# Reciprocals of softmax sums: two VectorE transposes, or 128x32 numbers and small DMAs

## The chip, the cores and the metric

The kernel runs on one NeuronCore of one Trainium2 chip. The metric is device time in microseconds (us) of one execution, the median of the runs. Five engines work side by side, each through its own list of instructions in order: TensorE (PE in the profile, with its weight loads as PEld), VectorE (DVE), ScalarE (ACT), GpSimd (POOL) and SyncE (SP). SP computes nothing here: it issues nearly all DMAs, one after the other, and an issue that has to wait holds up every issue behind it.

## The reference

Two independent parts, joined along the last axis.

```
a: qkv = x @ wqkv                       x (2048, 576), 32 heads of 18
   scores = q.k / sqrt(18), key j allowed for query i if 0 <= i - j < 256
   o = softmax(scores) @ v
   a = concat_heads(o) @ wo
b: K = real part of sum over n of C * exp(dt*A*l) * dt*B     (576 channels, 2048 taps)
   b = causal convolution of u (2048, 576) with K along the sequence + u * Dskip
out = concat([a, b], -1)                (2048, 1152)
```

What matters here is the division in the softmax: each head and query has one sum of exponentials, and the 18 numbers of that head's output are divided by it.

## The kernel before, in words

The kernel is written as *streams*, Python generators named by a letter, and the order of all work is a string in `PLAN`. One letter runs the next step of a stream; a letter with a digit runs the next posted continuation of that kind. Every engine executes its instructions in the order in which the string makes them, and the semaphore waits between engines follow from which tile each step reads or writes. Nothing is reordered at run time. There are four strings: `front` and `tables` (projection of q, k, v and the taps of the convolution), `first`, and `rest`, in which attention, the convolution by its spectra and the output projection are interleaved. The change is in `rest`.

Attention works on 16 *items*, item i = 4c + o being a block c of 512 queries and a group o of 8 heads. Per item:

- `aload` (stream L, `load`): SP loads Q, K and V of an item from DRAM into one of three sets of buffers. This is done for item i + 3 once item i has been through `o_out`.
- `smax` (stream s): 16 score tiles for the row maximum on PE (L836, and the mask L844), each reduced by DVE (`red`, L870). The 16 columns are transposed on PE (L852), scaled by DVE into `m16` (L856), and four small DMAs of 2 KB (L863) write them into a row of the Q tile, so that the following score matmuls subtract the maximum.
- `scores` (stream a): the scores again, with that row (L921) and the mask (L930), and the exponential by ACT (L936).
- `pv` (stream v): PE multiplies by V (L956). V carries a column of ones times a constant, so in each group of 32 output rows, rows 0 to 17 are a head's output and row 18 is its softmax sum. ACT copies the result to SBUF (`osb`, 128 x 1024, L966).
- `norm` (stream n): the division, as below, then a split into a high and a low half (L994, L998) and four stores to DRAM (`od`, L1003). Once the four items of a query block are stored, the stream `wo` loads them for the output projection.

PE, DVE and ACT share three PSUM slots (`ring`): a score tile holds one from its first matmul until DVE or ACT has read it. The convolution uses the same slots: loads `tx` and `tk` (stream k, L660), spectra on PE (L675), products on DVE (L690, L691) and POOL (L696, L697), inverse on PE (L708), stores `h` (L721), reloads `hp` (L758) and a last transform (L769).

The division before: for each item DVE transposes all of `osb` in 32x32 blocks (L981), which puts the 32 sums of each partition into column 18; takes the reciprocal of that column, 128x32 numbers (L983); and transposes a broadcast of the reciprocals back (L985), so that every row of a group of 32 has the group's reciprocals. POOL multiplies (L990).

Of the kernel before, what the change touches and what calls it, by code (L numbers as in the profile page):

```python
# [10 lines left out]
F32 = mybir.dt.float32  # L11
# [31 lines left out]
def constants():  # L43
# [23 lines left out]
    for nm, v in mult.items():  # L67
# [40 lines left out]
        "a1vc2asaa1a1s6Lavva1sc3aa1ss2s2svs2ss4saa1s2s2ssas2s2sa1kss2s2nvvn3aa1kcc1aa1dc2sad1s2sksvs2s2a1v1cc"  # L108
        "1dc3dc2d4d1d1nc3cc1avc2ln1ksvs2vad4a1sn6ls2ss2a1vasaa1vs2Lla1ssvas6s2vsks2a1sdvss2as4n3n1s2d1sa1ac3s"
        "a1s2n6ss2ss2lan4d4a1ss2vsvv1ss2s2as2a1ss2vcc1c2ss2dd1aa1sc3s2svsLaa1s2vs2ala1vsaa1ss6sss2s2vas2ss2ss"  # L110
        "2vna1n3kn4aaa1a1vcvc1s4c2ass2a1vaa1vsd4ssv1s2s2s2aa1n1sc3vsss2s2s2Ldcnd1ac1c2dvd4a1sss2d1akva1sd4s2s"
        "2vd4asc3a1s2dslld1s6kn6ss4sas2s2svs2a1ss2savs2ss2a1sas2vd4a1sass2n3s2va1n1n6ss2sas2vsa1as2a1ss2ss2vL"
        "cllv1c1aaa1a1vvc2ss2ss2fakva1aa1sfavss6a1c3ee1s2saa1s2dcd1e4vvnc1c2aavvc3a1sa1s2s4aasfvs2kla1a1slvs2"
        "v1Ln4n4cc1c2elsve1vs2ss2asa1s2saa1ss2ss2asn3s2a1ss2s2ss2ss2svvalc3s2cn1lla1c1aa1ad4nvvc2n3ssa1ss6as2"
        "s2a1vss2as4ssve4a1s2ss2avs2asa1a1ds2svad1s2a1n6ssc3s2s2sas2sv1a1vvaas2a1a1snn3s2vvdss2d1asss2s2a1fvk"
        "kLcc1d4c2vaa1dd1sss6n4s2ass2va1aa1ess2ve1ss4s2ss2avn1ss2a1d4ass2ss2vLa1sn6ss2c3ekv1ss2s2sn1s2e1asa1s"
        "2sss2s2van4a1cdc1and1vvc2sac3va1s2ss6n3ss2a1saas2sa1a1s2svskvn1ss2as2d4svs2s2a1sas4s2n6sa1vs2assa1vv"
        "s2sd4s2s2ss2v1aaa1a1sss2s2n4vaa1svs2alLa1ss6dn6d1cc1vaa1vnan3c2va1c3ss2aa1s4ss2sss2s2svs2aa1svss2aws"
        "a1s2vase4s2aa1s2a1vvn4se4v1cs2c1aaa1vvc2a1Lsks2savsn1s2s2ss2a1kasvsd4a1s2aa1s2c3vssss6s2avss2ss2s2a1"
        "dsas2s4vd1saa1a1s2svss2s2ss2aan6vn4sa1a1svs2sLs2dsv1s2sd1s2s2asd4s2va1aavsa1aa1a1vs2cc1nd4vc2aavva1s"  # L120
        "sfs6s2fa1an3ea1e1cc1navkc3ln3s4a1c2n1en6e1ss2vsss2n1s2ss2vaa1sc3s2vv1sas2a1dd1ava1ncac1c2dc3va1kaLsd"
        "1aa1a1vs2ss2vaka1ss2svss2s2asvs2ss2a1n6n4asvs2a1sava1s2ss6lss2cc1s4svslvv1s2c2sas2a1d4fd4ln3sls2ss2s"
        "s2s2asas2a1a1e4ssss2s2s2aa1Lsvn4ss2s2savn1vks2safs2a1vasa1a1s2ndd1ss6s4ee1d4ss2vsasa1s2vn6asc3s2s2la"
        "1svs2cdc1d1c2ss2sas2e4sn3n1a1vsas2s2aa1va1ss2ss2c3d4vkss2e4av1sn6van4s2a1svaa1a1s2lsss2vs2clc1c2dd1e"
        "sd4ae1s6vkna1cc1c3c2vadvaa1d1c3a1cvc1vawn3n1n6s4wa1c2w1aa1aa1dc3avd4a1vv1n4n4de4d1vvnd1d4d4aaa1a1waa"
        "1w4wwww1w4w1wwffww1w4aaa1vva1ee1e4ee1faavva1n3w4a1aa1www1wwwww4wwvvw1w4fn1n6w1vvv1ee4nn3w1e1w4wn1ee1"
        "n4ww4www1w4wn6n4wwww1w4w1wwww4e4e4ww1ww4w1wwwww4w1w4w1w4ww1w4",
# [3 lines left out]
class Kernel:  # L131
# [108 lines left out]
    def prep(self):  # L240
        nc, t, sp, tp = self.nc, self.t, self.p["tabc"], self.p["prep"]
        self.halfpi = sp.tile([128, 1], F32, name="halfpi")
        nc.vector.memset(self.halfpi, math.pi / 2)
        src, T, h, r = {}, {}, {}, {}
        for n in ("re", "im"):
# [538 lines left out]
    def att_setup(self):  # L784
        nc, a, ap = self.nc, self.a, self.p["att"]
# [12 lines left out]
        self.od = self.p["dram"].tile([4, 288, 2, 2, 512], F16, name="od")  # L798
        self.loaded = self.maxed = self.ndone = 0
# [174 lines left out]
    def norm(self):  # L974
        nc, np_ = self.nc, self.p["n"]
        for i in range(16):
            c, o = divmod(i, 4)
            yield "DVE", lambda: (self.osb[i],), lambda: i in self.osb and self.ndone >= i - 1
            osb = self.osb[i]
            T = np_.tile([128, 32, 32], F32, name="T")  # L980
            nc.vector.transpose(T.rearrange("p k r -> p (k r)"), osb.rearrange("p z c -> p (z c)"))  # L981
            R = np_.tile([128, 32], F32, name="R")
            nc.vector.reciprocal(R, T[:, :, 18])  # L983
            rb = np_.tile([128, 2, 512], F32, name="T")
# [218 lines left out]
```

## Time and profile before

| | us |
|---|---|
| median of 3 runs | 883.62 (881.54 to 885.16) |
| the profiled execution, its own time | 884.13 |
| its span, first to last instruction | 882.3 |
| PE busy in the span | 724.2 (82%) |
| DVE busy | 599.7 (68%) |
| ACT busy | 522.7 (59%) |
| POOL busy | 378.0 (43%) |
| mean granted TensorE clock | 0.92 |

The profile lists each engine's busy time, groups of equal instructions with what ended the idle time ahead of them, the waits by who waited for whom, and a chain: the work that ended last, followed back from the end, each piece to what released it. A row of a timeline gives the start, the length, the engine, the line, the operation and the tiles; a bracket at its end is the idle time before it and what ended that. SP's rows (SPq) are issues: the length is that of the issue, not of the transfer.

### The profile page before, as it was taken

The page shows a single profiled execution, that of the slowest core. Times are in us where ns is not written, and L with a number is a line of the kernel's source. Part 1 is how long each engine was busy: PE and PEld are TensorE (multiplying, and loading weights), DVE is VectorE, ACT ScalarE, POOL GpSimd, SP SyncE. Part 2 cuts the span into 40 slices and gives each one's busy share as a digit, 9 for nine tenths or more (in the row PEclk, how much of TensorE's full clock was granted, in tenths as well). Part 3 has the DMA queues.
Part 4 walks back from the last instruction along what each step waited for, and adds up shares of the span by engine and source line. Part 5 has one row for each costly group of instructions (what it writes and reads, how often), then busy time and mean ns, then how long its engine had stood idle before and what let it go on. Part 6 is the DMA issues. An engine that isn't in the chain of part 4 may idle for free.

```text
span 882.3 us, 32024 instructions
## 1 busy us (share of the span) xinstructions
PE 724.2 (82%) x14234; PEld 440.0 (50%) x14234; DVE 599.7 (68%) x798; ACT 522.7 (59%) x685; POOL 378.0 (43%) x295
## 2 busy tenths in 40 slices
PE   4565957998889789886888888887998987999977
PEld 2321523456446545454555554455555554567655
DVE  5855887887987787768657796575876767861010
ACT  3247676678777857671455566555766666676421
POOL 2256867766687655665015142221332042432020
PEclk9885969999999999996889999869999999999998
DMA  9795261546247745458549667637639573846743
GB/s 310 256 230 137 61 160 34 141 100 175 63 106 199 152 116 161 99 158 233 145 147 293 212 212 232 163 103 240 204 120 270 166 227 116 264 144 181 236 143 129
DMA packets 211051, 150.85 MB, mean 171 GB/s; under 512 B 102698, under 2 KB 191530, under 8 KB 210656
## 3 DMA queue, kind: packets, MB, share of 16 engines
q1 hardware_dynamic: 208896, 144.80, 58.5%
q0 software_dynamic: 2016, 3.99, 1.5%
q8 instruction: 112, 1.84, 0.9%
q14 instruction: 27, 0.22, 0.1%
HBM read 83.50 MB, written 65.11 MB: 168 GB/s over the span
## 4 chain that ended last, share of the span: by engine, by line
PE 46%; DVE 17%; ACT 12%; issue 10%; DMA 6%; SPq 4%; POOL 4%; ACTq 0%; DVEq 0%; POOLq 0%
PE pp L178 9%; PE po L956 7%; PE ring L178 6%; DVE m L870 5%; ACT P L936 4%; PE ring L708 4%; PE ring L921 4%; PE ring L836 3%; PE ring L675 3%; PE ring L575 2%; PE ring L453 2%; PE ring L769 2%; PE ring L465 2%; DMA K<-kz 1%; DVE m L552 1%
## 5 line engine op out<-in xcount | busy, mean ns | idle before, releaser
L870 DVE TENSOR_REDUCE m<-ring 128x2 f32<-128x640 f32 (+4 forms) x256 | 187.7, 779 | 66.6 <-PE ring L844 61.5
L936 ACT ACTIVATE P<-ring,esc 128x1024 f32<-128x1024 f32 (+2 forms) x160 | 166.8, 1060 | 102.3 <-PE ring L930 91.7
L546 POOL TENSOR_TENSOR m<-A,tr 128x1024 f32<-128x1024 f32 x72 | 144.0, 2017 | 79.2 <-DVE m L552 66.7
L956 PE MATMUL po<-P,V 64*32 64x320 f32 (+4 forms) x2816 | 105.7, 369 | 6.3 <-issue 6.3
L836 PE MATMUL ring<-K,Q 54*64 54x320 f16 (+4 forms) x1024 | 82.3, 322 | 26.5 <-DMA K<-kz 8.6
L696 POOL TENSOR_TENSOR Y<-t,t 128x384 f32<-128x384 f32 x24 | 24.0, 998 | 139.2 <-DVE t L691 133.3
L990 POOL TENSOR_TENSOR osb<-osb,T 128x1024 f32<-128x1024 f32 x16 | 37.8, 2362 | 100.6 <-DVE T L985 80.9
L921 PE MATMUL ring<-Q,K 55*64 55x320 f16 (+4 forms) x1408 | 67.7, 270 | 14.1 <-ACT P L936 3.4
L836 PEld LDWEIGHTS <-Q 54*64 54x64 f16 x1024 | 42.8, 109 | 71.7 <-issue 63.4
L998 POOL TENSOR_TENSOR oh<-osb,oh 128x1024 f16<-128x1024 f32 x16 | 34.1, 2130 | 73.5 <-ACT oh L994 73.5
L178 PE MATMUL pp<-xh,wh 128*128 128x512 f16 x180 | 48.6, 401 | 19.0 <-ACT vst L365 9.6
L178 PEld LDWEIGHTS <-wh 128*128 128x128 f16 x324 | 31.7, 101 | 57.1 <-issue 17.6
L844 PE MATMUL ring<-sm,idb 64*64 64x128 bf16 x896 | 56.9, 229 | 1.5 <-issue 1.5
L552 DVE TENSOR_TENSOR m<-m,m 128x1024 f32<-128x1024 f32 x36 | 53.3, 1480 | 4.8 <-POOL m L546 4.7
L956 PEld LDWEIGHTS po<-P,V 64*32 64x32 f32 x2816 | 39.1, 108 | 34.5 <-issue 25.0
L575 PE MATMUL ring<-Q,m 128*32 128x64 f32 x2304 | 42.6, 231 | 16.1 <-DVE m L552 13.4
L921 PEld LDWEIGHTS <-K 55*64 55x64 f16 x1408 | 33.8, 110 | 42.7 <-issue 34.0
L575 PEld LDWEIGHTS ring<-Q,m 128*32 128x32 f32 x2304 | 37.0, 117 | 29.8 <-issue 12.6
L178 PE MATMUL pp<-xh,wl 128*128 128x512 f16 x180 | 49.9, 412 | 0.0
L981 DVE STREAM_TRANSPOSE T<-osb 128x1024 f32<-128x1024 f32 x16 | 19.8, 1235 | 42.7 <-ACT osb L966 42.7
L930 PE MATMUL ring<-tm,idb 64*64 64x128 bf16 (+1 forms) x1152 | 44.9, 213 | 2.9 <-issue 2.9
L527 POOL TENSOR_TENSOR tr<-tr,mab 128x768 f32<-128x768 f32 x18 | 33.6, 1867 | 31.2 <-ACT tr L522 31.1
(162 smaller groups left out, 1570.2 us busy)
## 6 DMA issues: line engine op xcount, KB each, us to landing
gx<-ust SPq DMA_DIRECT2D x16, 576.0 KB
gk<-kst SPq DMA_DIRECT2D x18, 512.0 KB
tx<-gx SPq DMA_DIRECT2D x24, 384.0 KB
tk<-gk SPq DMA_DIRECT2D x24, 384.0 KB
h<-ho SPq DMA_DIRECT2D x48, 192.0 KB
hp<-h SPq DMA_DIRECT2D x12, 768.0 KB
Q<-qz SPq DMA_DIRECT2D x16, 512.0 KB
K<-kz SPq DMA_DIRECT2D x16, 512.0 KB
```

The source lines that it names most:

```text
L178: self.nc.tensor.matmul(ps, u, v, start=(i == 0), stop=(i == len(ops) - 1))
L546: tt(m[part], A[:, ch, a0:a0 + 8].unsqueeze(3).to_broadcast(sh), tr[:, ch, part, 0:8].unsqueeze(2).to_broadcast(sh), op=OP.mult)
L552: self.nc.vector.tensor_tensor(m[0], m[0], m[1], op=OP.add)
L575: nc.tensor.matmul(kp[32 * st:32 * st + 32, j, :], m[:, ch, 32 * term:32 * term + 32], Q[:, ch, term, :], start=(term == 0), stop=(term == ...
L836: nc.tensor.matmul(ps[z:z + 64, b, :n], d["Q"][rr, 2 * b + pp, 64 * qb:64 * qb + 64], d["K"][rr, 2 * b + pp, k0:k1], start=True, stop=Fals ...
L844: nc.tensor.matmul(out, self.idb[rr], self.sm[rr], start=False, stop=True, skip_group_check=True)
L870: self.nc.vector.tensor_reduce(out, x, axis=AX.X, op=OP.max)
L921: nc.tensor.matmul(ps[z:z + 64, b, off:off + w], d["K"][rr, 2 * b + pp, kc:kc + 64], d["Q"][rr, 2 * b + pp, q0:q0 + w], start=(k == 0), st ...
L930: nc.tensor.matmul(ps[z:z + 64, b, 64 * blk:64 * blk + w], self.idb[rr], self.tm[rr, self.MO[kinds]:self.MO[kinds] + w], start=False, stop ...
L936: nc.scalar.activation(P[:, :, lo:hi], ps[:, :, lo:hi], AF.Exp, scale=self.esc)
L956: nc.tensor.matmul(po[32 * p:32 * p + 32, z, q0:q0 + w], V[64 * z:64 * z + 64, kb * 76 + 19 * p:kb * 76 + 19 * p + 32], P[p % 2][64 * z:64 ...
L990: nc.gpsimd.tensor_tensor(osb, osb, rb, op=OP.mult)
```

## The change

For items 0 to 13 (`LR = 14`) the two transposes go. In their place:

1. SP reads row 18 of each group of 32 rows of `osb` by a DMA into a tile `R` of 128x32: 128 pieces of 128 bytes (L986). It is the step `n`, and it waits for ACT's copy into `osb`.
2. DVE takes the reciprocal of `R` in place (step `n5`, L1000).
3. SP stores `R` to DRAM, a row of `rden` of its own for each item (step `n7`, L1003).
4. SP reads each of that row's four parts back, broadcast to 18 partitions, into one tile `rb`, four DMAs of 18 x 4 KB (step `n8`, L1008). They wait until the store has landed, and until POOL has finished with the `rb` of the item before.
5. POOL multiplies `osb` by `rb` as before (step `n3`).

`rb` is one tile for all items, filled with ones at the start by POOL, since rows 18 to 31 of a group are never written. Items 14 and 15 keep the transposes. In the string `rest` only the steps of stream n are moved or added; all other steps keep their order. For items 0 to 13 `n` now stands 1 to 98 steps earlier than before, and the new steps follow it at a distance of some 10, 2 and 8 other steps.

```diff
-        "a1vc2asaa1a1s6Lavva1sc3aa1ss2s2svs2ss4saa1s2s2ssas2s2sa1kss2s2nvvn3aa1kcc1aa1dc2sad1s2sksvs2s2a1v1cc"
+        "a1nvc2asaa1a1s6Lavvn5a1sn7c3aa1ss2s2svn8s2ss4saa1s2s2ssas2s2sa1kss2s2vvn3aa1kcc1aa1dc2sad1s2sksvs2s2"
...
+        self.rden = self.p["dram"].tile([self.LR, 4, 1024], F32, name="rden")
+        self.rb = ap.tile([128, 1024], F32, name="rb")
+        nc.gpsimd.memset(self.rb, 1.0)
...
             osb = self.osb[i]
+            R = np_.tile([128, 32], F32, name="R")
+            if i < self.LR:
+                nc.sync.dma_start(R, osb.rearrange("(p r) z (k c) -> r p (z k) c", r=32, c=32)[18])
+                self.post("5", (R,), lambda i=i, osb=osb, R=R: self.spread(i, osb, R))
+                continue
             T = np_.tile([128, 32, 32], F32, name="T")
             nc.vector.transpose(T.rearrange("p k r -> p (k r)"), osb.rearrange("p z c -> p (z c)"))
-            R = np_.tile([128, 32], F32, name="R")
             nc.vector.reciprocal(R, T[:, :, 18])
             rb = np_.tile([128, 2, 512], F32, name="T")
             nc.vector.transpose(rb.rearrange("p z (k r) -> p (z k) r", r=32), R.unsqueeze(2).to_broadcast([128, 32, 32]))
             self.post("3", (rb,), lambda i=i, osb=osb, rb=rb: self.norm2(i, osb, rb))
+
+    LR = 14
+
+    def spread(self, i, osb, R):
+        nc, rb, row = self.nc, self.rb, self.rden[i]
+        nc.vector.reciprocal(R, R)
+
+        def out():
+            nc.sync.dma_start(row.rearrange("p (k c) -> (p k) c", c=32), R)
+            self.post("8", (R,), back)
+
+        def back():
+            for p in range(4):
+                nc.sync.dma_start(rb[32 * p:32 * p + 18], row[p:p + 1].partition_broadcast(18))
+            self.post("3", (rb,), lambda: self.norm2(i, osb, rb.rearrange("p (z c) -> p z c", z=2)))
+        self.post("7", (R,), out)
```

What this does to the lists of instructions is seen best at three places. Lines after the setup are higher in the changed kernel: its L810, L811, L813, L816 are the loads of Q, K (two of them) and V, its L867 the maxima's small DMAs, its L661 the loads of `tx` and `tk`, its L722 the stores of `h`, its L1042 a load of weights, its L874 the reduce, L691 and L692 the products, L860 the scaling to `m16`. `Q_4388`, `Q_4392`, `Q_4396` are the Q buffers of the three sets, and the same set's K follows its Q.

SP, item 0, before (loads for item 3, then the maxima of item 2):

```order
L660 DMA tk<-gk 128x4x192
L806 DMA Q_4388<-qz 128x2048
L807 DMA K_4389<-kz 128x4x512
L812 DMA V_4390<-vd 128x608
L863 DMA Q_4396<-m_5645 1x16x64 x4
L660 DMA tx<-gx 128x4x192
```

and now:

```order
L661 DMA tk<-gk 128x4x192
L986 DMA R<-osb 128x1x32
L810 DMA Q_4388<-qz 128x2048
L811 DMA K_4389<-kz 128x4x512
L816 DMA V_4390<-vd 128x608
L1003 DMA rden<-R 128x32
L1008 DMA rb<-rden 18x1024 x4
L867 DMA Q_4396<-m_5650 1x16x64 x4
L661 DMA tx<-gx 128x4x192
```

The read of the sums stands ahead of the three loads, and the store and the four broadcasts ahead of the maxima of item 2.

DVE, items 0 and 1, before (the products of the convolution, the reduces, the transposes):

```order
L856 TENSOR_SCALAR m_5645<-ring 32x128
L870 TENSOR_REDUCE m<-ring 128x2 x9
L981 STREAM_TRANSPOSE T<-osb 128x1024
L983 RECIPROCAL R<-T 128x32
L985 STREAM_TRANSPOSE T<-R 128x1024
L690 TENSOR_TENSOR t_5950<-X,ring 128x768
L691 TENSOR_TENSOR t_5951<-X,ring 128x768
L870 TENSOR_REDUCE m<-ring 128x2 x3
L690 TENSOR_TENSOR t_6084<-X,ring 128x768
L691 TENSOR_TENSOR t_6085<-X,ring 128x768
L981 STREAM_TRANSPOSE T<-osb 128x1024
```

and now:

```order
L860 TENSOR_SCALAR m_5650<-ring 32x128
L1000 RECIPROCAL R<-R 128x32
L874 TENSOR_REDUCE m<-ring 128x2 x9
L691 TENSOR_TENSOR t_5955<-X,ring 128x768
L692 TENSOR_TENSOR t_5956<-X,ring 128x768
L874 TENSOR_REDUCE m<-ring 128x2 x3
L691 TENSOR_TENSOR t_6089<-X,ring 128x768
L692 TENSOR_TENSOR t_6090<-X,ring 128x768
L691 TENSOR_TENSOR t_6158<-X,ring 128x768
L692 TENSOR_TENSOR t_6159<-X,ring 128x768
L1000 RECIPROCAL R<-R 128x32
```

Item 0's reciprocal stands right behind `m16` of item 2; item 1's behind one more pair of products than its transposes did.

SP, item 1, before (a weight load, then the loads for item 4):

```order
L721 DMA h<-ho 128x2x192 x2
L1018 DMA wraw_6226<-in_wo_dram 128x720
L806 DMA Q_4392<-qz 128x2048
L807 DMA K_4393<-kz 128x4x512
L809 DMA K_4393<-kz 128x4x256
L812 DMA V_4394<-vd 128x912
```

and now:

```order
L1003 DMA rden<-R 128x32
L722 DMA h<-ho 128x2x192 x2
L1042 DMA wraw_6229<-in_wo_dram 128x720
L1008 DMA rb<-rden 18x1024 x4
L810 DMA Q_4392<-qz 128x2048
L811 DMA K_4393<-kz 128x4x512
L813 DMA K_4393<-kz 128x4x256
L816 DMA V_4394<-vd 128x912
```

The loads for item 4 now stand behind the store and the broadcasts of item 1.

SP, item 6, before (`hp`, two rounds of convolution loads, the loads for item 9):

```order
L780 DMA out_dram<-y 64x4x192 x2
L758 DMA hp<-h 128x8x192
L660 DMA tx<-gx 128x4x192
L660 DMA tk<-gk 128x4x192
L660 DMA tx<-gx 128x4x192
L660 DMA tk<-gk 128x4x192
L806 DMA Q_4388<-qz 128x2048
```

and now:

```order
L781 DMA out_dram<-y 64x4x192 x2
L986 DMA R<-osb 128x1x32
L1003 DMA rden<-R 128x32
L759 DMA hp<-h 128x8x192
L661 DMA tx<-gx 128x4x192
L661 DMA tk<-gk 128x4x192
L661 DMA tx<-gx 128x4x192
L661 DMA tk<-gk 128x4x192
L810 DMA Q_4388<-qz 128x2048
```

Here the read of the sums and the store of the reciprocals follow each other directly, ahead of five loads.

More of the change, by code (lines that the diff above doesn't have):

```diff
@@ L112 @@
[L112 to L126, printed above, removed]
@@ L128 @@
+        "ww1w4aaa1vva1ee1e4ee1faavva1n3w4a1aa1www1wwwww4wwvvw1w4fn1n6w1vvv1ee4nn3w1e1w4wn1ee1n4ww4www1w4wn6n4"
+        "wwww1w4w1wwww4e4e4ww1ww4w1wwwww4w1w4w1w4ww1w4",
 }
```

22 lines of the change are left out of this document (18 added, 4 removed).

## The prediction

> **What bounds the kernel now.** I read the busy times by stretch first, then the chain of waits, then the timelines of SP, DVE and PE around the steps that move. The steps concerned run from 450 to 785 us, and this is most of that stretch:
>
> ```profile
> 430.00:760.00 330.00, 281.16 (x8058) 171.21 (x8050) 241.72 (x321) 199.33 (x208) 92.26 (x65) 0.94 0.67 200
> ```
>
> After its length come the busy times of PE, PEld, DVE, ACT and POOL. PE has 281 of 330 us. DVE has 242, so it is not the bound; what it delays is a PE that finds no free `ring` slot. PE's own rows in the list of waits give the size of that:
>
> ```profile
> PE ring L836 <- DVE m L870: 3.9, 15, 0.4
> PE ring L921 <- DVE t L691: 2.9, 3, 1.4
> ```
>
> Some 7 us in all, whatever the reason DVE was late. PE executes a fixed list, so a tile that arrives late stops all of it; the question is whether the new waits on SP make tiles late.
>
> **What the change removes.** By the groups of instructions on `T`, each transposed item costs DVE 1.23 + 0.35 + 1.25 = 2.83 us:
>
> ```profile
> L981 DVE STREAM_TRANSPOSE T<-osb x16: 1221/1234/1246, 463.9 to 838.6; 128x1024 f32<-128x1024 f32 x16
> L983 DVE RECIPROCAL R<-T x16: 353/354/356, 465.2 to 839.8; 128x32 f32<-128x32 f32 x16
> L985 DVE STREAM_TRANSPOSE T<-R x16: 1245/1245/1247, 465.6 to 840.2; 128x1024 f32<-128x1024 f32 x16
> ```
>
> The reciprocal stays at about 0.35 us (same size, contiguous instead of strided), so 14 items free 14 x 2.48 = 35 us of DVE. What counts is how much stood on the chain:
>
> ```profile
> 510.07 1.16 DVE T L981
> 511.64 0.49 DVE T L985
> ...
> 586.16 1.16 DVE T L981
> 587.73 0.86 DVE T L985
> ...
> 632.25 1.16 DVE T L981
> 633.83 0.36 DVE T L985
> ...
> 783.44 1.16 DVE T L981
> ```
>
> Four items (2, 5, 7, 13), 6.35 us, and four reciprocals of 0.36 between them: 7.8 us. Elsewhere other work hid the transposes. When they go, the next-longest chain takes over part of it. The gain is between 0 and 7.8 us; I take 6, nearer the chain's own rows.
>
> **What the change adds: prices.** The trace has no DMA of 128 rows by 128 bytes with its landing, but small ones on the same queue appear in the chain, from issue to the work they released, and so do two large loads. Two groups of SP's issues give the issue time (shortest, median, longest):
>
> ```profile
> 594.02 1.87 DMA Q<-m
> ...
> 740.63 4.02 DMA Q<-m
> ...
> 478.82 6.72 DMA K<-kz
> ...
> 461.45 4.21 DMA tk<-gk
> ...
> L863 SPq DMA_DIRECT2D Q<-m x64: 502/587/1515, 414.6 to 787.0; - x64
> L1003 SPq DMA_DIRECT2D od<-oh x64: 264/316/1262, 489.9 to 848.3; - x64
> ```
>
> A small DMA lands 1.87 to 4.02 us after its issue; I take 3.0, the middle, for the read into `R` and for the store to `rden`. The four broadcasts have the shape of the `od` stores (18 rows of 4 KB), so 4 x 0.32 = 1.3 us to issue. The other new issues take 0.3 to 0.6 us. All 84 issues make 84 x 0.32 to 0.59 = 27 to 50 us of SP's time over some 330 us; SP has that on average, and I put nothing for it beside the places below.
>
> The Trainium skill, page "DMA: Bandwidth & Descriptors", section "Anatomy of one DMA — SWDGE (gpsimd) path", puts the fixed cost of a DMA at about 2.0 us, mostly the confirmation that the last byte has landed, from a fit on another issuing path. The small DMAs above agree at their lower end (1.87) and not at their upper (4.02). With 2.0 for 3.0 the sum below would be an estimate of about 6 us smaller.
>
> What the new waits cost depends on the places. `n5`, the reciprocal, stands at a fixed place in DVE's list; `n7` (store) waits for it on SP; `n8` (broadcasts) waits there for the store to land. Everything behind them on SP waits too. I set each place's rows beside the new order.
>
> *Item 0.* The copy into `osb` is early; the reciprocal now stands behind `m16` of item 2 (L856), and that item's maxima behind the broadcasts:
>
> ```profile
> 450.64 1.02 ACT L966 ACTIVATE osb<-po 128x1024 f32<-128x1024 f32 x1
> ...
> 457.38 0.28 DVE L856 TENSOR_SCALAR m<-ring 32x128 f16<-32x128 f32 x1 [0.38 <-PE ring L852]
> ...
> 457.69 3.04 SPq L863 DMA_DIRECT2D Q<-m  x4
> ...
> 461.79 0.50 PE L921 MATMUL ring<-Q,K 55*64 55x64 f16 x12
> ```
>
> SP issues the maxima the moment `m16` is done, and PE starts item 2's scores 4.1 us later, about what such a DMA takes: no slack. Between `m16` and the maxima come 0.35 (reciprocal) + 3.0 (store lands) + 1.3 (broadcasts) = 4.7 us, all of it PE's. Ends 3.5 and 5.7.
>
> *Item 1.* The reciprocal stands behind the pair of products that ends at 480.83; the loads of K for item 4 stand behind the broadcasts:
>
> ```profile
> 479.88 0.95 DVE L691 TENSOR_TENSOR t<-X,ring 128x768 f32<-128x768 f32 x1
> ...
> 477.37 0.43 SPq L806 DMA_DIRECT2D Q<-qz  x1
> 478.16 0.60 SPq L807 DMA_DIRECT2D K<-kz  x1
> 478.82 0.62 SPq L809 DMA_DIRECT2D K<-kz  x1
> ...
> 485.63 0.33 PE L836 MATMUL ring<-K,Q 54*64 54x320 f16 x4 [0.16 <-DMA K<-kz]
> ```
>
> K already arrives 0.16 us late. New issue of its second part: 480.83 + 0.35 + 3.0 + 1.3, and 1.2 for Q and K ahead of it, is 486.7 in place of 478.82: 7.9 us later, of which I count 7.8. Ends 6.7 and 8.9.
>
> *Item 2.* Store, then the loads for item 5, behind a reciprocal that follows the reduce at 500.41:
>
> ```profile
> 500.41 0.82 DVE L870 TENSOR_REDUCE m<-ring 128x2 f32<-128x640 f32 x1
> ...
> 494.44 0.63 SPq L809 DMA_DIRECT2D K<-kz  x1
> ...
> 505.83 0.31 PE L836 MATMUL ring<-K,Q 54*64 54x320 f16 x4
> ```
>
> Reciprocal done at 501.6, store and two loads issued, K's second part at 503.0, landed 6.7 later at 509.7, needed at 505.83: 3.5 rounded down, since loads also land faster. Ends 1.5 and 4.
>
> *Item 6.* The store waits for a reciprocal behind the second of three reduces that start at 610.12, so until 611.3, with five loads behind it:
>
> ```profile
> 610.12 2.52 DVE L870 TENSOR_REDUCE m<-ring 128x2 f32<-128x640 f32 x3 [2.75 <-PE ring L844]
> ...
> 597.55 0.50 SPq L660 DMA_DIRECT2D tk<-gk  x1
> ...
> 612.42 0.50 PE L675 MATMUL ring<-tk,w 64*32 64x192 f32 x7
> ```
>
> `tk` was issued at 597.55, 15 us ahead of its use; it now goes out at 612.8 and lands by the row of 4.21 us at 617: 4.5 us late. Ends 2.5 and 6.
>
> *Items 5, 10, 12.* Here reads or other streams are held:
>
> ```profile
> 579.10 0.34 SPq L1036 DMA_DIRECT2D orow<-omx  x1
> ...
> 576.31 2.52 DVE L870 TENSOR_REDUCE m<-ring 128x2 f32<-128x640 f32 x3 [4.82 <-PE ring L844]
> ...
> 702.28 0.98 SPq L758 DMA_DIRECT2D hp<-h  x2
> ...
> 749.80 0.75 SPq L809 DMA_DIRECT2D K<-kz  x1
> ...
> 759.56 0.33 PE L836 MATMUL ring<-K,Q 54*64 54x320 f16 x4
> ```
>
> Item 5: its read stands behind `orow`, so `R` lands at 579.5 + 3 = 582.5, while DVE reaches the reciprocal among the reduces at 578 and stands for 4.5 us with PE's slots full behind it; part falls in idle time there: 3 (ends 0 and 4.5). Item 10: the `h` stores that `hp` reads back stand behind a store that waits for DVE: 2.5 (ends 0 and 4). Item 12: Q and K of item 15 stand behind the broadcasts; the second K goes out about 5.6 us after 749.80 and lands at 762.1, needed at 759.56: 2.5 (ends 0 and 4).
>
> *Other items, and the rest.* At items 3, 4, 7, 8, 9, 11 and 13 the same working ends within the slack that the loads have: 0, with 1 us each as the upper end. POOL's multiply waits for `rb` up to 9 us longer at item 1, but POOL is busy 92 of 330 us and PE stands there for K anyway: 0. The fill of `rb` at the start is one POOL operation on 128x1024; POOL has room: 0.
>
> Sum: 4.7 + 7.8 + 3.5 + 4.5 + 3 + 2.5 + 2.5 = 28.5, less 6, is +22.5 us. The profiled execution took 884.13 (span 882.3, and 1.8 around it), 0.06% above the median 883.62; 884.1 + 22.5 gives **907 us**. All lower ends with the full gain: 14.2 - 7.8 = +6.4, 890.5. All upper ends without gain: 37.1 + 7 = +44, 928.
>
> **Rivals.** *Faster: SP has the slack.* SP often stands waiting for DVE itself, and what is behind those waits would not notice:
>
> ```profile
> SPq L863 <- DVE m L856: 61.6, 11, 10.3
> ```
>
> If the new waits fall into such time, only the freed DVE time counts: 884.1 - 6 = 878, down to 876 with the whole 7.8 us. Against it: at items 0 and 1 the very thing behind the wait is what PE needs next. It decides from the point where all places together cost PE under 6 us, less than item 1 alone in my count.
>
> *Partly absorbed.* The places do cost, but a late PE gives the next loads slack, and one place pays for several: two places out of seven, say items 0 and 1 at their lower ends, 10.2 - 6 = +4 us, 888.
>
> *Worse.* The large loads ahead of the store in the queue delay its landing as they delay each other (6.72 us for K against 1.87 for a small one). With 6.7 in place of 3.0 at items 0, 1 and 12, where the store must land before the loads go, and 3.7 more at three of the items I put at 0: 907 + 6 x 3.7 = 929.
>
> *No effect from the DVE side.* That the transposes do go is settled by the order of the instructions; that they were hidden is the gain's lower end, and leaves 913.
>
> **How the numbers follow.** I give 0.64 to the forecast (890.5 to 928), 0.09 to the absorbed case, 0.06 to nearly nothing at all, 0.14 to the faster rival and 0.07 to the worse one. About 0.5% (4.4 us) is what a measurement can tell from no change, so faster means below 879.2 and slower above 888. The absorbed case lies at that bound, half to each side. Faster 0.14, same 0.06 + 0.04 = 0.10, slower 0.64 + 0.05 + 0.07 = 0.76. The range of 8 in 10 goes from 881 to 930: it leaves out nearly all of the faster rival and half of the worse one.
>
> **What would show it.** DVE busy lower by some 35 us over the span; DVE no more in the chain with T. In the chain, rows of `rden` and `rb`, and waits of PE on `Q<-m` and `K<-kz` of several us near items 0 and 1, against 0.2 to 4 now. PE's busy time in us unchanged and its share lower. SP's own waits: L1008 on the landing of `rden`, L1003 on DVE's L1000. The forecast is wrong if the scores of item 2 and the first tile of item 4 start as closely behind their loads as now without PE having stood still, or if `R` and `rden` land in under 2 us everywhere.

## The result and the profile after

The changed kernel takes 936.85 us (median of 4 runs, 933.45 to 938.53) against 882.58 for the kernel before on the same chip: ratio 1.061, 95% interval 1.056 to 1.066. It is slower, as forecast, but by 54 us where 22.5 were forecast (907 us), and above the range of 881 to 930. The profiled execution took 936.20 us with a span of 933.8, 51.5 us more than the 882.3 before.

The busy times on the changed kernel's page:

```profile
PE 737.5 (79%) x14234; PEld 448.2 (48%) x14234; DVE 568.1 (61%) x770; ACT 522.7 (56%) x685; POOL 378.6 (41%) x296
```

Against 599.7 before, DVE is relieved of 31.6 us. PE is idle for 933.8 - 737.5 = 196.3 us where it was 882.3 - 724.2 = 158.1: 38.2 us more. And the same 14234 matmuls are busy for 13.3 us longer. These two make the 51.5.

SP's waits between 430 and 860 us, where the items lie (total, times, longest):

```profile
SPq L1003 <- DVE R L1000: 38.5, 11, 6.6
SPq L986 <- ACT osb L970: 32.7, 8, 6.5
...
SPq L1008 <- DMA rden<-R: 27.5, 9, 5.2
...
SPq L867 <- DVE m L860: 8.3, 3, 6.1
```

The first three are new, 98.7 us. They took the place of most of SP's old wait for the maxima's `m16` (61.6 us before, 8.3 now), and some 45 us of them are time that SP did not stand before. PE's waits in the same stretch name what came late:

```profile
PE ring L840 <- DMA K<-kz: 16.4, 5, 7.2
PE ring L925 <- DVE m L874: 8.7, 6, 7.0
...
PE ring L676 <- DMA tx<-gx: 6.6, 2, 5.8
...
PE ring L925 <- DMA Q<-m: 4.6, 8, 1.1
PE ring L840 <- DMA h<-ho: 2.3, 1, 2.3
```

PE's timeline has these stops at the forecast places. The bracket gives the idle time before the row and what ended it:

```profile
462.09 0.63 PE L925 MATMUL ring<-Q,K 55*64 55x64 f16 x3 [0.60 <-DMA Q<-m]
...
494.02 0.48 PE L840 MATMUL ring<-K,Q 54*64 54x320 f16 x4 [7.24 <-DMA K<-kz]
...
519.14 0.48 PE L840 MATMUL ring<-K,Q 54*64 54x320 f16 x4 [4.42 <-DMA K<-kz]
...
603.01 0.64 PE L925 MATMUL ring<-Q,K 55*64 55x256 f16 x8 [6.99 <-DVE m L874]
...
637.85 1.54 PE L676 MATMUL ring<-tx,w 64*32 64x192 f32 x32 [5.77 <-DMA tx<-gx]
```

In order these belong to items 0, 1, 2, 5 and 6. The second row is the one that stood at 485.63 before, with 0.16 us of waiting and a length of 0.33 us. Behind the stop the same four matmuls take 0.48. The stretches around it show the clock (after the length: busy times, then the granted clock, the DMA share and GB/s):

```profile
480.00:486.00 6.00, 5.26 (x162) 2.83 (x170) 4.79 (x7) 2.36 (x4) 2.14 (x1) 1.00 0.36 96
486.00:494.00 8.00, 0.78 (x17) 0.18 (x18) 1.25 (x3) 0.79 (x1) 3.38 (x3) 0.69 1.02 290
494.00:497.00 3.00, 2.98 (x52) 1.45 (x52) 1.02 (x2) 0.79 (x1) 0.86 (x1) 0.50 1.10 336
497.00:500.00 3.00, 3.00 (x56) 2.12 (x52) 1.36 (x2) 0.24 (x1) 0.00 (x0) 0.61 0.69 205
500.00:503.00 3.00, 1.93 (x73) 1.48 (x66) 2.77 (x4) 2.69 (x4) 0.00 (x0) 1.00 0.26 87
```

After the 7.24 us stop PE works 6 us at a clock of 0.50 to 0.61 and loses 1.4 us more: set against the kernel before, instruction by instruction, it is 8.4 us behind at the first tile and 9.8 us behind at 500 us. The Trainium skill, page "TensorE: Matmul & The Clock Gate", section "What's actually happening", says that the clock is halved after an idle window of about 3.4 us and comes back after as long of work. For this stop the trace agrees roughly: the clock is still at 0.50 in the first 3 us of work and back at 1.00 from 6 us on. Stops shorter than that window were followed by the lower clock too (last section), and there the measurement decides.

### The profile page after: what moved, and what is told of

Its sections match the earlier page's. It is cut to its first block, busy times and chain, and to the rows that moved or that the text cites. A ratio compares the mean times of both kernels' runs of the same rounds, so it can differ in the third digit from the quotient of the medians.

```text
span 933.8 us, 32131 instructions
## 1 busy us (share of the span) xinstructions
PE 737.5 (79%) x14234; PEld 448.2 (48%) x14234; DVE 568.1 (61%) x770; ACT 522.7 (56%) x685; POOL 378.6 (41%) x296
## 4 chain that ended last, share of the span: by engine, by line
PE 37%; DMA 17%; DVE 14%; ACT 11%; issue 10%; SPq 7%; POOL 3%; ACTq 0%; DVEq 0%; POOLq 0%
PE pp L179 8%; PE ring L179 6%; PE po L960 4%; ACT P L940 3%; PE ring L709 3%; PE ring L925 3%; DMA K<-kz 3%; PE ring L676 2%; PE ring L840 2%; DMA Q<-m 2%; DVE m L874 2%; PE ring L454 2%; PE ring L576 2%; SPq L867 2%; PE ring L466 2%
## 5 line engine op out<-in xcount | busy, mean ns | idle before, releaser
L874 DVE TENSOR_REDUCE m<-ring 128x2 f32<-128x640 f32 (+4 forms) x256 | 187.0, 778 | 86.5 <-PE ring L848 79.6
L840 PE MATMUL ring<-K,Q 54*64 54x320 f16 (+4 forms) x1024 | 84.2, 332 | 46.7 <-DMA K<-kz 23.6
L925 PE MATMUL ring<-Q,K 55*64 55x320 f16 (+4 forms) x1408 | 69.8, 274 | 24.8 <-DVE m L874 8.7
L1014 POOL TENSOR_TENSOR osb<-osb,rb 128x1024 f32<-128x1024 f32 x14 | 33.0, 2360 | 104.5 <-DMA rb<-rden 54.0
L691 DVE TENSOR_TENSOR t<-X,ring 128x768 f32<-128x768 f32 x24 | 22.9, 954 | 68.0 <-PE ring L676 32.8
L179 PE MATMUL pp<-xh,wl 128*128 128x512 f16 x180 | 47.6, 397 | 0.0
```

What stands on the lines that cost most here:

```text
L179: self.nc.tensor.matmul(ps, u, v, start=(i == 0), stop=(i == len(ops) - 1))
L840: nc.tensor.matmul(ps[z:z + 64, b, :n], d["Q"][rr, 2 * b + pp, 64 * qb:64 * qb + 64], d["K"][rr, 2 * b + pp, k0:k1], start=True, stop=Fals ...
L874: self.nc.vector.tensor_reduce(out, x, axis=AX.X, op=OP.max)
L925: nc.tensor.matmul(ps[z:z + 64, b, off:off + w], d["K"][rr, 2 * b + pp, kc:kc + 64], d["Q"][rr, 2 * b + pp, q0:q0 + w], start=(k == 0), st ...
```

## The experiments

The microseconds below are the ratio to the kernel before on the same chip, less one, times 882.6; by this measure the whole change costs 53.5 (interval 49.1 to 58.0). In code, L1000 and so on are the lines of the changed kernel.

### Is the relief worth anything, and is it waits or traffic?

No small DMA and no transposes:

```diff
-                nc.sync.dma_start(R, osb.rearrange("(p r) z (k c) -> r p (z k) c", r=32, c=32)[18])
-        nc.vector.reciprocal(R, R)
+        nc.vector.reciprocal(self.Rc, self.Rc)
-            nc.sync.dma_start(row.rearrange("p (k c) -> (p k) c", c=32), R)
-            for p in range(4):
-                nc.sync.dma_start(rb[32 * p:32 * p + 18], row[p:p + 1].partition_broadcast(18))
```

> Leaves out, for items 0 to 13, the division by the softmax sums: no small DMA is issued, no transpose is made, the reciprocal works on a constant tile and the product takes ones. So VectorE is relieved as in the change, and nothing is asked of SP. My theory (the gain is the 6 us by which the chain of waits of before stood on transposes, the loss is all SP's): 876 to 882 us against 883 before. Rival (VectorE's work was covered by TensorE and gives nothing): 883. Rival (the lower clock comes from the change of VectorE's work, not from SP): well over 883, and the granted clock near 0.90 as in the changed kernel; by my theory it is 0.92.

Measured: 886.91, ratio 1.0024 (0.9983 to 1.0064), +2.1 us. Its page:

```profile
PE 721.3 (81%) x14234; PEld 439.9 (50%) x14234; DVE 568.7 (64%) x770; ACT 522.5 (59%) x685; POOL 378.3 (43%) x297
```

DVE is relieved as in the change, and the time does not fall. The gain of 6 us, read off four items in the chain, was not there: the interval allows at most 1.5 us. With the other steps at these places, no cheaper way to the reciprocals can gain more than that here, by this interval.

All 84 small DMAs, with no copy, reciprocal or landing to wait for:

```diff
-                nc.sync.dma_start(R, osb.rearrange(...)[18])
+                nc.sync.dma_start(R, self.oc.rearrange(...)[18])
-        nc.vector.reciprocal(R, R)
+        nc.vector.reciprocal(self.Rd, self.Rd)
-            nc.sync.dma_start(row.rearrange(...), R)
+            nc.sync.dma_start(row.rearrange(...), self.Rc)
-                nc.sync.dma_start(rb[32 * p:32 * p + 18], row[p:p + 1].partition_broadcast(18))
+                nc.sync.dma_start(rb[32 * p:32 * p + 18], self.r0[p:p + 1].partition_broadcast(18))
```

> Leaves out the division by the softmax sums for items 0 to 13, but issues all 84 small DMAs at their places on SP's queue with their sizes and addresses alike: the reads take a constant tile, the stores a constant tile, the broadcasts a row written once at the start, and the reciprocal a tile of its own. So SP has the issues and the chip has the traffic, and no wait for a copy of ScalarE's, a reciprocal or a landing. My theory (SP waits, and what is queued behind it comes late): 878 to 890 us, at most 10 us over the kernel without the small DMAs. Rival (the traffic or the time that SP takes to issue 84 DMAs): 920 to 937.

Measured: 887.76, ratio 1.005 (1.001 to 1.010), +4.6 us. Issue time and traffic cost 0.4 to 8.7 us, beside 53.5. The rest is waits, of SP and of DVE.

### Whose waits?

The six small DMAs per item from GpSimd's queue (in all three places):

```diff
-                nc.sync.dma_start(R, ...)
+                nc.gpsimd.dma_start(R, ...)
```

> The changed kernel with its six small DMAs per item issued by GpSimd's queue in place of SP's, at the same places of the program; the output is the whole one. SP's queue is that of before, without waits for reciprocals and landings. My theory (the cost is what stands behind the waiting issues on SP): the late loads of K, Q and h go, GpSimd's own waits delay its products and subtractions, of which little waits, and VectorE still waits for R where it did (3 times, 11.6 us): 885 to 900 us. Rival (traffic, or the late normalisation itself, costs the time): 925 to 940. Rival (GpSimd's queue holds up work that TensorE waits for as SP's did): 910 to 940, with waits of TensorE on GpSimd's tiles in the profile.

Measured: 899.78, ratio 1.018 (1.012 to 1.025), +16.1 us. Some 37 of the 53.5 us (by some 7 us either way) are SP's queue. The Trainium skill, page "DMA: Bandwidth & Descriptors", section "Issuing engines are not separate DMA queues", says that issuing from several engines only saves the sequencer's time. Here the move saved far more than issue time and traffic together can cost (at most 8.7 us, above): the other queue has the same kind of waits, but no loads behind them. Then GpSimd's queue and, besides, no wait of DVE for R:

```diff
-        nc.vector.reciprocal(R, R)
+        nc.vector.reciprocal(self.Rc, self.Rc)
-            nc.gpsimd.dma_start(row.rearrange(...), R)
+            nc.gpsimd.dma_start(row.rearrange(...), self.Rc)
```

> Leaves out the division for items 0 to 13: the small DMAs are issued by GpSimd's queue, and the reciprocal and the store take a constant tile, so that VectorE never waits for R. With both waits away the change would cost little: my theory 884 to 893 (GpSimd's queue alone gave 899.8, and taking VectorE's stand away from the changed kernel gave 13 us by the ratios). Rival (what was left of the cost on GpSimd's queue is the late products and h of GpSimd): 896 to 902.

Measured: 896.06, ratio 1.019 (1.013 to 1.025), +16.9 us. My theory (884 to 893) fell: with the DMAs on GpSimd, DVE's wait for R is worth nothing that these runs can tell. What is left fits the rival, late work of GpSimd, but isn't shown to be that: some 5 us of it may be issue and traffic (4.6 above). In the profile of the former kernel GpSimd's waits are

```profile
POOL rden L1003 <- DVE R L1000: 64.2, 10, 11.5
...
POOL rb L1008 <- DMA rden<-R: 33.4, 12, 5.6
```

with its products and subtractions behind them (from 430 to 860 us). Which of these PE pays for was not taken further.

Each wait alone, on SP's queue as in the change. DVE's wait for R, by the same edit as just now on SP:

> Leaves out the division for items 0 to 13: the reciprocal takes a constant tile in place of R, and the store stores that tile. VectorE then never waits for the landing of R; SP still waits for ScalarE's copy, for VectorE's reciprocal at its place, and for the landing of the stored row. In the changed kernel VectorE stood 11.6 us for R in three places (10.0 of them at item 5), and TensorE 7.0 us behind that. My theory (the prediction's term for item 5, 3 us, was too small: it cost about 9, and without it SP's store of that item goes out earlier too): 923 to 929 against 937. Rival (VectorE's stand hides what comes late anyway): 934 to 938.

SP's wait for the reciprocal:

```diff
-            nc.sync.dma_start(row.rearrange(...), R)
+            nc.sync.dma_start(row.rearrange(...), self.Rc)
```

> Leaves out the division for items 0 to 13: the store takes a constant tile, so that SP doesn't wait for VectorE's reciprocal (38.5 us in 11 places); the reciprocal of R still stands at its place on VectorE, and SP still waits for ScalarE's copy and for the landing of the row. My theory (the three waits of SP each stand for their part of the 37 us that went when the DMAs left SP's queue: 38.5 of 98.7): 14 us less, 920 to 926. Rival (the next wait takes its place: the broadcasts wait for the landing of the row wherever the store goes out): 932 to 938. VectorE's stand for R stays by both.

SP's wait for the landing of the row:

```diff
-                nc.sync.dma_start(rb[32 * p:32 * p + 18], row[p:p + 1].partition_broadcast(18))
+                nc.sync.dma_start(rb[32 * p:32 * p + 18], self.r0[p:p + 1].partition_broadcast(18))
```

> Leaves out the division for items 0 to 13: the four broadcasts read a row that was written once at the start, so that SP doesn't wait for the landing of the row (27.5 us in 9 places); it still waits for ScalarE's copy and for the reciprocal. My theory: 27.5 of 98.7 of the 37 us, so 10 us less, 924 to 930, with the maxima of item 2 back in time (the prediction put 4.7 on store and broadcasts there) and K of item 4 2 to 3 us earlier. Rival (the broadcasts lie behind a wait of SP that lasts as long): 934 to 938.

SP's wait for ACT's copy:

```diff
-                nc.sync.dma_start(R, osb.rearrange(...)[18])
+                nc.sync.dma_start(R, self.oc.rearrange(...)[18])
```

> Leaves out the division for items 0 to 13: the first small DMA reads a constant tile in place of ScalarE's copy, so that SP doesn't wait there for the copy (32.7 us in 8 places), and the read lands earlier, which takes VectorE's wait for R away too. My theory: 32.7 of 98.7 of the 37 us is 12, and VectorE's stand goes with it, some 9: 914 to 920. Rival (SP then waits longer for the reciprocal, which stands behind the copy on VectorE: the wait moves one place on): only VectorE's stand goes, 926 to 932.

| taken away | us, median | ratio (95%) | less than the 53.5, us |
|---|---|---|---|
| DVE's wait for R | 926.71 | 1.046 (1.040 to 1.051) | 13 |
| SP's wait for the reciprocal | 918.22 | 1.038 (1.033 to 1.044) | 20 |
| SP's wait for the landing | 929.83 | 1.052 (1.046 to 1.057) | 8 |
| SP's wait for the copy | 927.97 | 1.049 (1.043 to 1.054) | 11 |

Each difference in the last column is good to some 7 us. The wait for the reciprocal is worth more than that for the landing (no run of one reaches a run of the other); that either is worth more or less than its share of SP's waiting can't be told. The theories held for DVE's wait (923 to 929) and for the landing (924 to 930). For the reciprocal the time came out below both ranges (920 to 926, rival 932 to 938), and for the copy in the rival's (926 to 932). Part of a wait moves on, as the rivals of the last three runs said. SP's list of waits without the wait for the reciprocal shows that for the landing grown from 27.5:

```profile
SPq L1010 <- DMA rden<-Rc: 39.0, 10, 7.4
```

Without the wait for the copy, the list shows that for the reciprocal grown from 38.5:

```profile
SPq L1005 <- DVE R L1002: 70.7, 12, 12.0
```

So of 32.7 us of waiting for the copy almost all went into the next wait. The 11 us are not what the rival named, DVE's stand for R: that was 11.6 us in the changed kernel, and it is still there without the wait for the copy. What they are stays open. Of DVE's waits in that kernel:

```profile
DVE R L1002 <- DMA R<-oc: 12.2, 2, 10.9
```

### Which items?

The kernel with only some items in the new way (the others as before, at their old places in the order), first items 0 and 1:

```diff
-    LR = 14
+    LR = 2
```

> Only items 0 and 1 take the small DMAs, at their new places; items 2 to 15 are written as before. The output is the whole one. The prediction's terms for these two items are 4.7 (maxima of item 2 behind the store and the broadcasts) and 7.8 (K of item 4), 12.5 us together, and the part of the gain that lies in items 0 and 1 is none: 896 us, 893 to 900. The two profiles of before and after, put against each other, give 3.7 and 6.3, so 893. Rival (the loss is spread over all items, by traffic or by the clock): 14 items for 54 us, so 8 us for two: 891, with no wait for K of item 4.

Measured: 895.41, ratio 1.014 (1.008 to 1.021), +12.7 us. The forecast of 12.5 for these two items holds. At the first tile of item 4 PE stands for K, whose second part goes out at 486.36, where the prediction had it (486.7). PE's timeline of this kernel:

```profile
493.62 0.48 PE L839 MATMUL ring<-K,Q 54*64 54x320 f16 x4 [8.40 <-DMA K<-kz]
```

and in SP's timeline of the same kernel K's second part goes out:

```profile
486.36 0.62 SPq L812 DMA_DIRECT2D K<-kz  x1
```

Items 2 to 6:

```diff
-            if i < self.LR:
+            if 2 <= i < 7:
```

> Only items 2 to 6 take the small DMAs, at their new places; the others are written as before, and the output is the whole one. The prediction gave these items 3.5 (item 2), 3 (item 5) and 4.5 (item 6), less about 3 of the gain: 8 us. TensorE's lag behind the kernel before, read instruction by instruction from the two profiles, grows from 8 to 30 us over these items. My theory by now (VectorE's stand at item 5, the loads of items 3 to 6 and a slower TensorE between them cost what the lag shows, and the parts add): 22 us, 900 to 909. Rival (the items only cost so much because the first two had used up the slack): 890 to 898.

Measured: 905.87, ratio 1.030 (1.024 to 1.036), +26.4 us, as my theory had it.

Items 7 to 13:

```diff
-            if i < self.LR:
+            if 7 <= i < 14:
```

> Only items 7 to 13 take the small DMAs, at their new places; the others are written as before, and the output is the whole one. The prediction gave these items 2.5 (item 10) and 2.5 (item 12), less about 3 of the gain: 2 us. The lag grows from 30 to 50 us over them. My theory: 20 us, 898 to 907, and with two items (12.7) and items 2 to 6 (22) the three parts add up to the 54 of the whole change. Rival (a part alone costs much less than in company): 885 to 895.

Measured: 895.18, ratio 1.018 (1.014 to 1.023), +16.2 us, under the 20 of my theory. The three parts make 12.7 + 26.4 + 16.2 = 55.3 us, the whole 53.5; the sum is good to some 9 us, the whole to some 5. Within that the cost adds by places. Single items of the middle part, by the same edit with `if i == 3:`, and then 5 and 6:

> Only item 3 takes the small DMAs, at its new places; the output is the whole one. The prediction gave this item 0, with 1 as its upper end. In the profile with items 2 to 6 two stores of h stand behind the store of its row and land late, TensorE waits 3.0 us for ScalarE's copy of ho that needs their buffer, and the lag grows by about 5, of which some 2 go again. My theory: 3 to 6 us more than before. Rival (only late because item 2 made it so): 0 to 1 us.

Measured: 887.53, ratio 1.0055 (1.0021 to 1.0089), +4.9 us. Of PE's waits in its profile:

```profile
PE ring L924 <- ACT ho L715: 3.8, 2, 3.4
```

What held SP here is the read of the sums, which waits 7.4 us, the last 4.4 of them for ACT's copy. Behind it stand four loads, the store of the row and two stores of `h`. In SP's waits and timeline of this kernel:

```profile
SPq L985 <- ACT osb L969: 4.4, 1, 4.4
...
517.24 0.65 SPq L985 DMA_DIRECT2D R<-osb  x1
520.48 0.38 SPq L1002 DMA_DIRECT2D rden<-R  x1
520.91 1.18 SPq L721 DMA_DIRECT2D h<-ho  x2
```

The store of the row goes out the moment the loads are issued, so it waits for nothing. The two stores of `h` go out at 520.91, at 513.77 in the kernel before. Their buffers come free late, ACT's copy `ho` waits 4.8 us for them, and PE 3.4 us for that copy. The prediction had looked there only for loads, and only behind the store.

> Only item 5 takes the small DMAs, at its new places; the output is the whole one. The prediction gave 3 (VectorE stands for R, whose read goes out late behind the stores of an earlier item; 0 to 4.5). In the profile with items 2 to 6 TensorE waits 8.1 us for VectorE's maxima behind that stand, and the lag grows by 7.5. My theory now: 6 to 9 us more than before. Rival (the read is only late because the other items' small DMAs lie ahead of it): 0 to 3 us.

Measured: 889.58, ratio 1.004 (1.001 to 1.007), +3.7 us. My theory fell, and the prediction's 3 holds, though DVE and PE stand longer than its 4.5 us. Their rows in the list of waits of this kernel:

```profile
DVE R L999 <- DMA R<-osb: 11.7, 1, 11.7
...
PE ring L924 <- DVE m L873: 11.9, 5, 10.7
```

Some 4 us of the stop stand in the place of one in the profile of before, where PE waited for nothing that the profile shows:

```profile
574.84 0.90 PE L956 MATMUL po<-P,V 64*32 64x64 f32 x32 [4.14 <-issue]
```

Instruction by instruction against that profile, PE is level at 570 us, then 4.4 us ahead for want of that stop, and 5.7 us behind after its own; it is 9.1 us behind at 686 us and 4.5 us behind at 749 us.

> Only item 6 takes the small DMAs, at its new places; the output is the whole one. The prediction gave 4.5 (one spectrum load behind the store that waits for the reciprocal; range 2.5 to 6). In the profile with items 2 to 6 the lag grew by about 12 us here, with the loads of tx and tk, of Q, K and V of a later item and two stores of h all behind the same store. My theory now (everything that stands behind the waiting store counts, not only the first): 10 to 13 us more than before. Rival (the prediction's size): 3 to 6 us more.

Measured: 896.19, ratio 1.015 (1.011 to 1.020), +13.2 us, where 4.5 had been forecast. SP's timeline of this kernel:

```profile
603.25 0.64 SPq L985 DMA_DIRECT2D R<-osb  x1
609.57 0.35 SPq L1002 DMA_DIRECT2D rden<-R  x1
610.01 0.38 SPq L758 DMA_DIRECT2D hp<-h  x1
610.45 0.58 SPq L660 DMA_DIRECT2D tx<-gx  x1
611.08 0.50 SPq L660 DMA_DIRECT2D tk<-gk  x1
...
617.64 2.41 SPq L1007 DMA_DIRECT2D rb<-rden  x4
621.07 1.90 SPq L721 DMA_DIRECT2D h<-ho  x2
```

PE's waits in its profile from 595 to 660 us:

```profile
PE ring L675 <- DMA tx<-gx: 6.0, 1, 6.0
PE ring L839 <- DMA h<-ho: 2.6, 1, 2.6
```

The forecast's `tk`, out at 597.55 before, goes out at 611.08 (612.8 forecast). But the stop at these loads is 6.0 us, the stores of `h` behind them make a second one of 2.6, and between the two, from 616 to 619 us, PE has a clock of 0.50. The same with the store behind the loads (`n7` moved past `hp`, `tx`, `tk`, Q, K, V in the order, `n8` to its product):

> As with item 6 alone, but its store is issued behind the loads of tx, tk, Q, K and V that it held up, and its four broadcasts right ahead of their product on GpSimd; the read and the reciprocal stay where they are, and the output is the whole one. My theory (the cost lies in what is queued behind the waiting store): 0 to 3 us more than before. Rival (the cost lies in the reciprocal on VectorE or in the late product): as much as with item 6 alone, 10 to 13.

Measured: 890.57, ratio 1.0063 (1.0031 to 1.0095), +5.6 us. The two waits above are gone (`tx` from the rows, 2.7 us for `ho` in place of `h`), and more than half of the cost with them. The rest is more than my theory gave. The `ho` row is part of it. Another part may be the read, which stands ahead of the loads as before and waits for ACT's copy:

```profile
SPq L985 <- ACT osb L969: 6.9, 1, 6.9
...
604.93 0.50 SPq L660 DMA_DIRECT2D tk<-gk  x1
```

So `tk` still goes out 7 us later than the 597.55 of before. What that wait alone costs was not measured.

### Does another order repair the whole?

The letters of each item's steps moved: read 5 places later, reciprocal 8, store and broadcasts 11 to 14.

> All 14 items take the small DMAs, and the output is the whole one, but each step stands some places later in the order: the read of R 5, the reciprocal 8, the store and the broadcasts 11 to 14, so that most loads of K, V, Q, tx and tk are issued ahead of the stores that wait. My theory (what costs is the waiting in SP's queue, so a later place for the waiting issues takes most of it away): 892 to 910 against 937. Rival (the waits only move to the next loads, of which there are as many): 925 to 940.

Measured: 933.20, ratio 1.058 (1.053 to 1.064), +51.5 us: nearly nothing gained, as the rival had it. SP's waits in its profile:

```profile
SPq L1003 <- DVE R L1000: 38.7, 11, 7.5
SPq L986 <- ACT osb L970: 33.6, 7, 8.5
SPq L1008 <- DMA rden<-R: 20.8, 10, 3.8
```

Together they are nearly as long as before, 93.1 us for 98.7: SP had moved on through its list and waited at the new places as long as at the old. With more room (read 10 places later, reciprocal 20 behind it, store 25 behind that, broadcasts 15, product 16; items 0 to 12):

> As with the first stretched order, but each wait of SP gets more room, in items 0 to 12: the read stands 10 places later, the reciprocal 20 behind the read, the store 25 behind the reciprocal, the broadcasts 15 behind the store, the product 16 behind those; the output is the whole one. The first stretched order left SP's waits as long as they were (38.7, 33.6 and 20.8 us), since 5 places are some 2 us and SP runs further ahead of VectorE than that. My theory (a wait of SP goes only where the place of the issue is later than the work that it waits for): the three waits fall to less than half of the 93 us, and the time to 895 to 912. Rival (later stores and broadcasts hold up other loads, and late products hold up the rest): 920 to 940.

Measured: 903.99, ratio 1.022 (1.017 to 1.026), +19.1 us. SP's waits in its profile:

```profile
SPq L986 <- ACT osb L970: 10.2, 4, 4.5
SPq L1003 <- DVE R L1000: 8.9, 2, 5.5
SPq L1008 <- DMA rden<-R: 7.6, 4, 3.0
```

The three waits fall from 98.7 to 26.7 us and the cost from 53.5 to 19.1, with the same computation and the same DMAs. It is still slower than the kernel before, which fits a relief that is worth nothing.

### Stalls from another engine

The kernel before, with the first transpose made three times:

```diff
-            nc.vector.transpose(T.rearrange("p k r -> p (k r)"), osb.rearrange("p z c -> p (z c)"))
+            for _ in range(3):
+                nc.vector.transpose(T.rearrange("p k r -> p (k r)"), osb.rearrange("p z c -> p (z c)"))
```

> The kernel before, with the first of the two transposes made three times in each of the 16 items: 40 us more of work for VectorE at the places of the normalisation (32 transposes of 1.25 us), no DMA and no wait of SP added. It asks two things: whether the slack of VectorE, by which 32 us less of its work gained nothing, also takes 40 us more, and whether stalls of TensorE that come from VectorE lower the granted clock as those behind SP did. My theory: no slack upward, 15 to 30 us slower (898 to 913), TensorE's busy time up from 724 to some 732 and the clock down to 0.91. Rival (slack both ways): 883 to 888, clock 0.92. Rival (the clock falls by something else): slower by the stalls, with TensorE busy for 724 as before.

Measured: 906.46, ratio 1.031 (1.026 to 1.036), +27.4 us. The busy times on its page:

```profile
PE 728.5 (81%) x14234; PEld 441.8 (49%) x14234; DVE 638.3 (71%) x830; ACT 522.8 (58%) x685; POOL 378.0 (42%) x295
```

32 us of DVE's work taken away gave nothing, 40 us added cost 27, within my theory's 15 to 30. PE's busy time rose by 4.3 us, half of what I expected, with no DMA added.

## Why the prediction was right, and where it was wrong

The direction and the mechanism were right: SP's queue waits for a reciprocal and for a landing, loads behind it come late, PE stands. The size was wrong, and the time lies above the range, by these steps. The stops from item 2 on were priced too low: 11 us for items 2 to 6, which measured 26.4, and 5 us for items 7 to 13, which measured 16.2. Where single items were taken apart, the reasons seen are that only the first load behind the waiting store was counted, that stores of `h` were not, and that the read's wait for ACT's copy was put at nothing. A gain of 6 us was taken off that isn't there. And PE's busy time was put as unchanged, where it rose by 13.3 us at a lower clock.

The rival "SP has the slack" is partly true (some 50 us of the new waits replaced SP's old wait for `m16`), but far from enough. "Partly absorbed" is refuted by the parts, which add. "Worse" had nearly the time, 929, but not the cause: the landing's whole wait is worth 8 us, and what it blamed, a landing behind large loads, shows in the chain of the changed kernel as 5.29 us at most and 2.51 at item 0 (from issue to what it released):

```profile
455.56 2.51 DMA rden<-R
...
687.16 5.29 DMA rden<-R
```

By its terms:

- Items 0 and 1, 12.5: measured 12.7 (6.8 to 18.7). Right, each at its place: instruction by instruction PE's lag grows by 4.6 us at item 0 (4.7 forecast) and by 7.9 at item 1 (7.8 forecast). At item 0 the waits for the maxima are only 0.60 and 0.42 us, since PE came up to them at a clock of 0.50.
- Item 5, 3: measured 3.7 (0.9 to 6.5). Right on the time, and in part by luck: DVE stands 11.7 us for R where 4.5 were forecast, and some 4 us of PE's stop stand in the place of one that the profile of before has. The stop is 7 us long in the whole change and 10.65 with item 5 alone.
- Item 6, 4.5 (2.5 to 6): measured 13.2 (9.3 to 17.2). Mis-sized. I priced the first load behind the waiting store, and not the train behind that load, whose stores of `h` made a second stop. The reciprocal stands behind the first of the three reduces, not the second as written; the 611.3 of the sum is the time for the first.
- "Items 3, 4, 7, 8, 9, 11 and 13: 0": item 3 alone is 4.9 (1.9 to 7.9). I had held only loads against the slack, and only behind the store; here the read waits for ACT's copy, and what comes late is stores of `h`. Item 2, with item 4 and what the items of the middle part do to each other, is left with 26.4 - 4.9 - 3.7 - 13.2 = 4.6 (by some 8 us either way) for a forecast of 3.5.
- Items 10 and 12, 2.5 each, and none for the rest from 7 on: 16.2 (12.4 to 20.0) for the 5. Not measured item by item. In the profile of that part PE waits 4.4 us for `hp` at item 10, above its upper end of 4.
- The gain, 6 (0 to 7.8): none, at most 1.5. The likely reason, which no run isolates, is that a transpose in the chain is one of several paths of nearly the same length there; the chain shows only the last one.
- "PE's busy time in us unchanged": wrong, and no term of the sum stood for it. It rose by 13.3 us between the two profiled executions, as PE runs at half clock for some 5 us behind long stops. That is no fixed share of what is lost: with items 7 to 13 alone PE is busy for 723.4 us, no more than before, at a cost of 16.2.

Set against the spans: 22.5 forecast, 6 for the gain that was not there, 13.3 for the slower clock, and 9.7 that is left of the 51.5 for stops that were too small in the sum or missing from it.

Of the other signs to look for, most came out as written: DVE's busy time 31.6 us lower (35 forecast), no `T` in the chain for these items, rows of `rden` in it, PE's wait for K at item 4, and SP's waits at L1003 and L1008. The wait for the maxima of item 2 is not several us but 0.60 and 0.42, and the chain has no row of `rb`. The wait that I had not listed is SP's second largest, L986 for ACT's copy.

## What to carry to other kernels

A small DMA costs what stands behind it on the queue that issues it. Before a DMA that has to wait for a compute engine is put on a queue of loads that are issued ahead of their use, list everything that is issued behind it until the wait ends, stores included, and give the wait as much room in the order as the queue runs ahead (moving the steps 5 to 14 places later did nothing here that the runs can tell, moving them 10 to 50 places took most of the cost away). Whether taking work off an engine gains anything is tested more cheaply by a kernel that leaves the work out than read from a chain; and every long stop of TensorE should be priced with the slow microseconds behind it.

## What the runs showed of the hardware that was not expected

The granted clock tends to fall behind the stops. Over all runs its mean was 0.923 for the kernel before (73 runs) and 0.922 for the kernel without the small DMAs (10 runs), 0.911 for items 2 to 6, 0.910 for the added transposes, and 0.897 for the whole change (4 runs each), so it tends to go down with the time lost, whichever engine the stop comes from, but not in step: items 7 to 13 lost 16 us at 0.921. Stops well short of 7 us are followed by the lower clock too. These are stretches of the changed kernel behind a stop of 0.94 us for K that ends at 457.25 (item 0), behind the 4.42 us at item 2, the 6.99 us at item 5, and a stop of 1.16 us that ends at 800.73:

```profile
459.00:461.00 2.00, 1.97 (x52) 1.07 (x37) 0.89 (x2) 0.29 (x1) 0.00 (x0) 0.50 0.41 132
...
519.00:524.00 5.00, 4.65 (x108) 2.80 (x108) 3.84 (x5) 1.20 (x2) 0.55 (x1) 0.58 0.99 218
...
603.00:606.00 3.00, 2.85 (x48) 1.97 (x48) 3.00 (x5) 2.06 (x2) 0.00 (x0) 0.50 0.30 83
...
801.00:804.00 3.00, 2.94 (x105) 1.73 (x100) 2.38 (x3) 1.41 (x2) 0.00 (x0) 1.00 1.00 315
```

The first three are at 0.50, 0.58 and 0.50, the last at 1.00. So the length of the one stop doesn't decide: 0.94 us was followed by half clock, and 1.16 us was not. What does decide, no run here was made to show.
